# Clustered attention and two expert stages on one core: where the turned sums, the epsilon, the similarity transpose and the first weight conversions are issued

## The chip, the cores and the metric

The kernel runs on one core of one Trainium2 chip. The metric is the device time of one execution in microseconds, taken as the median of several runs. The engines have their usual names here: TensorE (PE, with PEld for its weight loads), VectorE (DVE), ScalarE (ACT), GpSimd (POOL) and SyncE (SP), whose queue issues the DMAs.

## The reference, cut to what matters

```python
B, H, S, D, clusters = 2, 8, 768, 64, 16
q_assign = argmax(einsum('bhsd,hcd->bhsc', q_n, c_n))     # the same for k
mask     = q_assign[..., None] == k_assign[..., None, :]
scores   = where(mask, q @ k.T / sqrt(D), -1e9)
attn     = exp(scores - max(scores))
attn     = attn / (sum(attn) + 1e-9)
x        = (attn @ v) as (1536, 512)
h        = ((x @ w1) * (x @ w2)) @ w3 @ w_out             # first expert stage
out      = (sigmoid(h @ w_gate) * (h @ w_val)) @ w_out2   # second expert stage
```

The weights arrive as 64-bit words and are turned into two-part 32-bit operands on the chip.

## The kernel before

Attention comes first and takes about the first third of the time. Its unit is the head pair: two heads of one batch element, so there are 8 pairs (`pr`, 0 to 7). A pair is cut into 6 blocks (`at`, 0 to 5), each of 256 queries of one head, and a block into two halves of 128 queries. One turn of the loop over `i` issues one block. It is a software pipeline: the turn of block `i` computes the score products of the tiles `2i+3` and `2i+4`, transposes the exponentials of block `i`, and makes the weighted sum of block `i-1`. The pair's twelve row sums come from the exponentials.

All engines run an order written out by hand (`manual_schedule`): each engine and each DMA queue executes what concerns it in the order of the calls in the loop's body, and waits where an operand or a buffer isn't ready. In each half of a block TensorE makes a score product (lines 312 to 315), transposes of exponentials (343) and weighted sums (384, 385). VectorE takes a row maximum (322) and makes the low parts of the transposed exponentials by a subtraction (372). ScalarE computes the exponentials (333), copies the high parts (361, or 358 where GpSimd makes the split, in blocks 1, 2 and 4), and moves a finished weighted sum out (393).

In PSUM there are two score tiles of 1024 columns, of which scores fill 768; three transpose tiles; and one tile for the weighted sum. The similarity product of a coming pair (`prep_sims`, line 242) borrows a score tile, and `rp`, the turned sums of a pair (line 412), a transpose tile.

Between these, the next pair is prepared a step at a time: similarities of queries and keys to the centroids (242), their transpose by VectorE (`prep_sum`, 248), the sum of their halves by GpSimd (`prep_add`, 254), maximum, code (267) and one-hot rows (274, 275), their transpose (279), and in block 3 `prep_mask`: GpSimd turns the key half into 0 or a large negative number (290), and SP moves the rows into QH and KH, the operands of the next pair's first score product, which is issued in the second half of block 4. Then GpSimd adds the head halves of the pair before (432), SP spreads its inverse sums, and GpSimd normalises in block 5. In blocks 3 and 4 the operands of the pair after the next are split (210, 212, 56, 59).

The pair's sums get an epsilon from ScalarE and a reciprocal from VectorE (`invert`, 407, 408, second half of block 4), a transpose by TensorE (`turn_sums`, 413, first half of block 5), and a copy and a store (`store_sums`, 419, 420, end of block 5).

The first four weight matrices (`w_f`, `w_a`, `w`) are converted during attention, each in four steps behind its load: ScalarE 93 and 94 with GpSimd 96; VectorE 102; VectorE 105 with GpSimd 106; ScalarE 108 with GpSimd 111. `CONVERT` says in which pair and block a step is issued, in all cases at the end of the block's second half. They are, as (pair, block): matrix 0 (1,1) (1,3) (1,5) (2,1); matrix 1 (2,3) (3,1) (3,3) (3,5); matrix 2 (4,1) (4,3) (4,5) (5,1); matrix 3 (5,3) (6,1) (6,3) (6,5).

Of the kernel before, what the change touches and what calls it, by code (L numbers as in the profile page):

```python
# [8 lines left out]
F32 = mybir.dt.float32  # L9
F32R = mybir.dt.float32r  # L10
U32 = mybir.dt.uint32
AF = mybir.ActivationFunctionType
# [3 lines left out]
B, H, S, D, C = 2, 8, 768, 64, 16  # L16
NP = H // 2
KT = S // 128
# [9 lines left out]
def tile_cluster_attention__then__moe__then__gated_moe(  # L28
# [15 lines left out]
    nc = tc.nc  # L44
# [4 lines left out]
    NPR = B * NP  # L49
# [69 lines left out]
    ps_t = att.enter_context(tc.tile_pool(name="ps_t", bufs=3, space=PSUM))  # L119
# [125 lines left out]
    def prep_sum(pr):  # L245
        sp = opnd.pop((pr, "sims"))
        sT = core.tile([128, S // 32, 32], F32, tag="raw", name=f"sT{pr}", bufs=3)
        nc.vector.transpose(out=sT.rearrange("p j c -> p (j c)"), in_=sp[:, 0:S])
        opnd[pr, "sT"] = sT
# [44 lines left out]
    def prep_v(pr, e):  # L294
        vx = core.tile([128, KT, 2, D], F32R, tag="vx", name=f"vx{pr}_{e}", bufs=3)
        split(raw[pr, "v"][:, e], vx[:, :, e, :], vx[:, :, 1 - e, :], nc.gpsimd, nc.gpsimd)
        opnd[pr, e, "v"] = vx
# [3 lines left out]
    NB = len(blocks)  # L301
    sps, nms, exps, pts, pcs, phs, avs, acc_x = {}, {}, {}, {}, {}, {}, {}, {}

    def scores(j):

        if not 0 <= j < 2 * NB:
            return
        pr, e, q0 = blocks[j // 2]
        QH, KH, QX, KX = opnd[pr, e]
        q = slice(q0 + 128 * (j % 2), q0 + 128 * (j % 2) + 128)  # L310
        sp = ps_s.tile([128, 1024], F32, tag="s", name=f"s{j}")
        nc.tensor.matmul(sp[:, 0:512], QH[:, q], KH[:, 0:512], start=True, stop=False)
        nc.tensor.matmul(sp[:, 512:S], QH[:, q], KH[:, 512:S], start=True, stop=False)
        nc.tensor.matmul(sp[:, 0:512], QX[:, q], KX[:, 0:512], start=False, stop=True)
        nc.tensor.matmul(sp[:, 512:S], QX[:, q], KX[:, 512:S], start=False, stop=True)  # L315
        sps[j] = sp

    def maxima(j):
        if j not in sps:
            return  # L320
        nms[j] = core.tile([128, 1], F32, tag="nm", name=f"nm{j}", bufs=4)
        nc.vector.tensor_reduce(out=nms[j], in_=sps[j][:, 0:S], axis=AX.X, op=ALU.max, negate=True)  # L322

    def exponentials(j):

        if j not in sps:
            return
        pr, e, q0 = blocks[j // 2]
        at = e * KT + q0 // 128 + j % 2
        if at == 0:  # L330
            acc_x[pr, "sum"] = core.tile([128, 2 * KT], F32, tag="ss", name=f"ss{pr}", bufs=2)
        et = core.tile([128, S], F32, tag="e", name=f"e{j}", bufs=5)
        nc.scalar.activation(et, sps.pop(j)[:, 0:S], AF.Exp, bias=nms.pop(j), accum_out=acc_x[pr, "sum"][:, at : at + 1])  # L333
        exps[j] = et
# [11 lines left out]
    def by_pool(i, k2):  # L346

        return k2 == 0 and i % 6 in (1, 2, 4)
# [15 lines left out]
    def split_lo(i, k2):  # L364
        if (i, k2) not in pts:
            return
        src = pts.pop((i, k2))
        ph, pl = phs[i, k2]
        if by_pool(i, k2):
            split(src, ph, pl, nc.gpsimd, nc.gpsimd)  # L370
        else:
            nc.vector.tensor_tensor(out=pl, in0=src, in1=ph, op=ALU.subtract)  # L372
# [31 lines left out]
    def invert(pr):  # L404

        ss = acc_x[pr, "sum"]
        nc.scalar.activation(ss, ss, AF.Copy, bias=1e-9)
        nc.vector.reciprocal(ss, ss)

    def turn_sums(pr):  # L410

        rp = ps_t.tile([128, 2, 256], F32, tag="t", name=f"rp{pr}")[0 : 2 * KT, 0, 0:128]
        nc.tensor.transpose(rp, acc_x.pop((pr, "sum")), ident)
        acc_x[pr, "rp"] = rp

    def store_sums(pr):
        rp = acc_x.pop((pr, "rp"))
        rt = core.tile([2 * KT, 128], F32, tag="rt", name=f"rt{pr}", bufs=1)
        nc.vector.tensor_copy(rt, rp)
        nc.sync.dma_start(r_dram[pr], rt)  # L420
# [75 lines left out]
    def convert(n):  # L496

        next(steps[n], None)

    CONVERT = {}  # L500
    slots = [(pr, at) for pr in range(1, NPR - 1) for at in ((1, 3, 5), (1, 3, 5), (1, 3))[pr % 3]]
    for n, slot in enumerate(slots[:16]):
        CONVERT[slot] = n // 4
    manual = ExitStack()
    manual.enter_context(tc.manual_schedule(engines={mybir.EngineType.PE, mybir.EngineType.DVE, mybir.EngineType.Activation, mybir.EngineType.Pool, mybir.EngineType.SP}))
    if True:
        for e in range(2):
            prep_v(0, e)
        for i in range(-2, NB + 2):
            pr, at = divmod(i, 6)  # L510
            nxt = pr + 1 if 0 <= i and pr + 1 < NPR else None
            later = nxt + 1 if nxt and nxt + 1 < NPR else None
            late = nxt == 1

            scores(2 * i + 3)
            split_hi(i - 1, 2)
            transposes(i, 0)
            if i == NB - 1:
                turn_sums(pr)
            maxima(2 * i + 3)  # L520
            if i == NB - 1:
                store_sums(pr)
            if nxt and at == 1 + late:
                prep_code(nxt)
            if nxt and at == 1:
                prep_scatter(nxt, 1)
            if later and at == 0:
                load_qk(later)
            if at == 2 and 0 < pr and i < NB:
                join_x(pr - 1)  # L530
            split_lo(i - 1, 2)
            split_hi(i, 0)
            split_lo(i, 0)
            if nxt and at == 3:
                for e in range(2):
                    prep_mask(nxt, e)
            if 0 < pr and i < NB and at == 5:
                norm_x(pr - 1)
                split_x(pr - 1)
            if nxt and at == 2:  # L540
                prep_v(nxt, 0)
            if 0 < pr and i < NB and at == 3:
                add_x(pr - 1)
                spread(pr - 1, "xb", 1)
            exponentials(2 * i + 3)
            if later and at == 3:
                halves = prep_split(later)
                next(halves)
            if later and at == 4:
                for _ in halves:  # L550
                    pass
            weighted_v(i - 1, 0)
            weighted_v(i - 1, 1)
            if 0 <= i < NB - 1 and at == 5:
                turn_sums(pr)
            if i == 0:
                prep_scatter(1, 0)
            if later and at == 5:
                prep_scatter(later, 0)
            if at == 0 and pr < 4:  # L560
                convert(pr)

            scores(2 * i + 4)
            if nxt and at == 0 and not late or i == 1:
                prep_add(nxt)
            if 0 < pr < NPR and at == 0:
                prep_v(pr, 1)
            if nxt and at == 0:
                load_v(nxt)
            transposes(i, 1)  # L570
            split_hi(i, 1)
            weighted_v(i - 1, 2)
            transposes(i, 2)
            take_x(i - 1)
            maxima(2 * i + 4)
            split_lo(i, 1)
            exponentials(2 * i + 4)
            if 0 <= i < NB and at == 4:
                invert(pr)
            if 0 <= i < NB - 1 and at == 5:  # L580
                store_sums(pr)
            if i == -2:
                halves = prep_split(1)
                next(halves)
            if i == -1:
                for _ in halves:
                    pass
            if i == 0:
                prep_sims(1)
                prep_sum(1)  # L590
            if nxt and at == late:
                prep_argmax(nxt)
            if nxt and at == 1 + late:
                prep_onehot(nxt)
            if nxt and at == 2:
                prep_turn(nxt)
            if (pr, at) in CONVERT:
                convert(CONVERT[pr, at])
            if later and at == 5:
                prep_sims(later)  # L600
                prep_sum(later)
            if i == NB - 2:
                end_move(0)
            if i == NB:
                end_move(1, FIRST)
                spread(END, "raw", 3)
                end_add(0)
        end_move(1, LAST)
        end_add(1, FIRST)
        end_norm(FIRST)  # L610
        end_split(FIRST)
        end_add(1, LAST)
        end_norm(LAST)
        end_split(LAST)
# [16 lines left out]
    slots = 0  # L631
# [10 lines left out]
    at = 0.0  # L642
# [118 lines left out]
    late, stage = {}, {}  # L761
# [268 lines left out]
    for M in range(MG // GS):  # L1030
        first = {5 + i: [(M - 1, i)] for i in range(6)} if M else {}
# [113 lines left out]
```

## Time and profile before

| | |
|---|---|
| time, median of 3 runs | 772.67 us (772.16 to 772.98) |
| the profiled execution's own time | 774.57 us |
| its span | 772.8 us |
| TensorE busy | 752.9 us, 97% |
| VectorE busy | 577.3 us, 75% |
| ScalarE busy | 468.9 us, 61% |
| GpSimd busy | 409.8 us, 53% |

The profile is of one execution. The span runs from its first to its last instruction. Busy shares are means over stages of different kinds: attention ends at about 248 us, and only there do VectorE and ScalarE come close to being full. Start times in a row are microseconds from the span's start. Square brackets at the end of a row tell how long the engine sat idle before the instruction and what released it.

### The profile page before, as it was taken

The numbers are of one execution on the slowest core, as the hardware profiler recorded it, in microseconds if no ns is written. First come the engines' busy times: TensorE is split into PE (matmuls) and PEld (weight loads), VectorE is DVE, ScalarE is ACT, GpSimd is POOL, SyncE is SP. The second block draws the span as 40 slices with busy tenths as digits, with TensorE's granted clock in tenths as the row PEclk, the third lists the DMA queues.
The fourth block names the chain that finished last, engine by engine and source line by source line (L and its number), as shares of the span: only waits on it lengthen the run. The fifth ranks groups of instructions, "written<-read, shape, count | busy, mean of one in ns | idle before, by whom it ended". The sixth has DMA issues, their size and how long they took to land.

```text
span 772.8 us, 12258 instructions
## 1 busy us (share of the span) xinstructions
PE 752.9 (97%) x4293; PEld 683.8 (88%) x4293; DVE 577.3 (75%) x895; ACT 468.9 (61%) x980; POOL 409.8 (53%) x418
## 2 busy tenths in 40 slices
PE   8899999999999999999999999899999999999998
PEld 7889888988998888888888999899999999999996
DVE  6799989998987666658663386757577877869674
ACT  2889788889796555455541354676756455564630
POOL 3447777877775355434231137574755647475520
PEclk9999999999999999999999999999999999999999
DMA  8867776756622443333330001130302213031004
GB/s 219 204 169 187 200 191 169 179 157 178 148 73 70 143 147 111 137 136 111 131 141 1 1 1 54 59 107 27 111 27 82 83 55 111 0 113 51 28 1 163
DMA packets 28894, 82.64 MB, mean 107 GB/s; under 512 B 4800, under 2 KB 4960, under 8 KB 28832
## 3 DMA queue, kind: packets, MB, share of 16 engines
q1 hardware_dynamic: 28832, 81.86, 35.6%
q8 instruction: 34, 0.56, 0.3%
q14 instruction: 28, 0.23, 0.1%
HBM read 52.49 MB, written 3.19 MB: 72 GB/s over the span
## 4 chain that ended last, share of the span: by engine, by line
PE 79%; DVE 8%; ACT 6%; issue 3%; POOL 2%; DMA 1%; SPq 0%; ACTq 0%; DVEq 0%; POOLq 0%
PE p L66 12%; PE p L67 12%; PE p L65 12%; PE pt L343 4%; PE p_a L65 4%; PE p_a L66 4%; PE p_a L67 4%; ACT e L333 2%; PE av L385 2%; DVE nm L322 2%; PE av L384 2%; PE p_b L65 2%; PE p_b L66 2%; PE p_b L67 2%; ACT ph L361 2%
## 5 line engine op out<-in xcount | busy, mean ns | idle before, releaser
L333 ACT ACTIVATE e<-s,nm 128x768 f32<-128x768 f32 x96 | 87.9, 916 | 17.3 <-DVE nm L322 15.8
L322 DVE TENSOR_REDUCE nm<-s 128x1 f32<-128x768 f32 x96 | 90.1, 939 | 4.5 <-PE s L315 4.5
L343 PE MATMUL pt<-ident,e 128*128 128x128 f32 x576 | 87.3, 275 | 2.4 <-DVE pl L372 2.4
L372 DVE TENSOR_TENSOR pl<-pt,ph 128x512 fp32r<-128x512 f32 x120 | 80.0, 682 | 10.0 <-ACT ph L361 8.0
L384 PE MATMUL av<-ph,vx 128*128 128x256 f32 x288 | 81.3, 308 | 0.1
L66 PE MATMUL p<-x,w 128*128 128x512 f32 (+1 forms) x208 | 80.0, 385 | 0.0
L65 PE MATMUL p<-x,w 128*128 128x512 f32 (+1 forms) x208 | 80.0, 385 | 0.0
L67 PE MATMUL p<-x,w 128*128 128x512 f32 (+1 forms) x208 | 80.0, 385 | 0.0
L361 ACT CAST ph<-pt 128x512 fp32r<-128x512 f32 x120 | 69.5, 598 | 15.8 <-PE pt L343 15.2
L385 PE MATMUL av<-pl,vx 128*128 128x256 f32 x288 | 74.7, 289 | 4.1 <-DVE pl L372 3.8
L343 PEld LDWEIGHTS pt<-ident,e 128*128 128x128 f32 x576 | 68.3, 142 | 8.4 <-PE s L315 4.2
L106 POOL TENSOR_TENSOR w_a<-w_f 128x512 uint32<-128x512 uint32 x32 | 34.8, 1086 | 62.1 <-DVE w_f L105 26.4
L1024 DVE TENSOR_TENSOR acc<-p,acc 128x512 f32<-128x512 f32 x60 | 41.2, 687 | 29.9 <-PE p L67 29.7
L931 ACT COPY s<-p_a 128x384 f32<-128x384 f32 x72 | 34.4, 480 | 44.2 <-PE p_a L67 43.9
L385 PEld LDWEIGHTS av<-pl,vx 128*128 128x128 f32 x288 | 54.6, 189 | 6.9 <-DVE pl L372 6.3
L855 POOL TENSOR_TENSOR wgv_a<-wgv_f 128x512 uint32<-128x512 uint32 x24 | 25.3, 1055 | 63.4 <-DVE wgv_f L854 43.2
L67 PE MATMUL p<-wo,u 128*128 128x512 f32 x144 | 57.0, 396 | 0.0
L66 PE MATMUL p<-wo,u 128*128 128x512 f32 x144 | 56.7, 394 | 0.0
L65 PE MATMUL p<-wo,u 128*128 128x512 f32 x144 | 56.0, 389 | 0.0
L384 PEld LDWEIGHTS av<-ph,vx 128*128 128x128 f32 x288 | 54.4, 189 | 1.4 <-issue 0.5
L65 PEld LDWEIGHTS p<-x,w 128*128 128x128 f32 x208 | 39.0, 188 | 7.5
L67 PEld LDWEIGHTS p<-x,w 128*128 128x128 f32 x208 | 39.0, 188 | 7.4
(232 smaller groups left out, 2304.3 us busy)
## 6 DMA issues: line engine op xcount, KB each, us to landing
wgv_f<-in_w_gv_dram SPq DMA_DIRECT2D x24, 512.0 KB, 3.2
wo_f<-in_w_out_dram SPq DMA_DIRECT2D x20, 512.0 KB, 3.3
w_f<-in_w_dram SPq DMA_DIRECT2D x16, 512.0 KB, 4.8
w_f<-in_w3T_dram SPq DMA_DIRECT2D x16, 512.0 KB, 3.9
raw<-in_qkT_dram SPq DMA_DIRECT2D x16, 384.0 KB, 3.2
vraw<-in_v_dram SPq DMA_DIRECT2D x8, 384.0 KB
QH<-hi SPq DMA_DIRECT2D x16, 192.0 KB, 4.5
KH<-hi SPq DMA_DIRECT2D x16, 192.0 KB, 3.7
```

The source lines that it names most:

```text
L65: nc.tensor.matmul(ps, whi, xhi, start=start, stop=False, skip_group_check=more)
L66: nc.tensor.matmul(ps, whi, xlo, start=False, stop=False, skip_group_check=more)
L67: nc.tensor.matmul(ps, wlo, xhi, start=False, stop=stop, skip_group_check=more)
L106: nc.gpsimd.tensor_tensor(out=a, in0=high, in1=low, op=ALU.add)
L322: nc.vector.tensor_reduce(out=nms[j], in_=sps[j][:, 0:S], axis=AX.X, op=ALU.max, negate=True)
L333: nc.scalar.activation(et, sps.pop(j)[:, 0:S], AF.Exp, bias=nms.pop(j), accum_out=acc_x[pr, "sum"][:, at : at + 1])
L343: nc.tensor.transpose(pt[:, kk, 128 * t : 128 * t + 128], exps[2 * i + t][:, k0 : k0 + 128], ident)
L361: nc.scalar.copy(ph, pt)
L372: nc.vector.tensor_tensor(out=pl, in0=src, in1=ph, op=ALU.subtract)
L384: nc.tensor.matmul(avs[i], w, ph[:, kk, :], start=kt == 0, stop=False)
L385: nc.tensor.matmul(avs[i], w, pl[:, kk, :], start=False, stop=kt == KT - 1)
L1024: nc.vector.tensor_tensor(out=acc[:, t, :], in0=bk, in1=acc[:, t, :], op=ALU.add)
```

## The change

`invert` is cut in two. The epsilon (`guard_sums`) is issued in the first half of block 4, behind that half's exponential, and the reciprocal stays in the second half. `turn_sums` gets its room from the caller: for all pairs but the last it is columns 768 to 895 of the score tile `2i+4`, and it is issued in the second half of block 5, behind that tile's score product; `store_sums` follows the maximum of that tile. The similarity transpose (`prep_sum`) moves from the end of the block of its product into the first half of the next block, behind the subtraction of the block before and ahead of the maximum. The conversion steps of matrix n are issued at (pair n+2, block 0, second half), (n+2, block 1, second half), (n+2, block 3, first half) and (n+3, block 2, first half). In a first half they stand behind the low part of the block's first transposes and ahead of `prep_mask` and `prep_v`.

```diff
     def invert(pr):
 
         ss = acc_x[pr, "sum"]
+        nc.vector.reciprocal(ss, ss)
+
+    def guard_sums(pr):
+        ss = acc_x[pr, "sum"]
         nc.scalar.activation(ss, ss, AF.Copy, bias=1e-9)
-        nc.vector.reciprocal(ss, ss)
-
-    def turn_sums(pr):
-
-        rp = ps_t.tile([128, 2, 256], F32, tag="t", name=f"rp{pr}")[0 : 2 * KT, 0, 0:128]
+
+    def turn_sums(pr, room):
+
+        rp = room[0 : 2 * KT]
         nc.tensor.transpose(rp, acc_x.pop((pr, "sum")), ident)
         acc_x[pr, "rp"] = rp
...
     CONVERT = {}
-    slots = [(pr, at) for pr in range(1, NPR - 1) for at in ((1, 3, 5), (1, 3, 5), (1, 3))[pr % 3]]
-    for n, slot in enumerate(slots[:16]):
-        CONVERT[slot] = n // 4
+    for n in range(4):
+        for slot in ((n + 2, 0, 1), (n + 2, 1, 1), (n + 2, 3, 0), (n + 3, 2, 0)):
+            CONVERT[slot] = n
...
             transposes(i, 0)
             if i == NB - 1:
-                turn_sums(pr)
+                turn_sums(pr, ps_t.tile([128, 2, 256], F32, tag="t", name=f"rp{pr}")[:, 0, 0:128])
+            first = nxt and at == late
+            if first:
+                split_lo(i - 1, 2)
+                prep_sum(nxt)
             maxima(2 * i + 3)
...
             split_lo(i - 1, 2)
             split_hi(i, 0)
             split_lo(i, 0)
+            if (pr, at, 0) in CONVERT:
+                convert(CONVERT[pr, at, 0])
             if nxt and at == 3:
                 for e in range(2):
                     prep_mask(nxt, e)
...
             exponentials(2 * i + 3)
+            if 0 <= i < NB and at == 4:
+                guard_sums(pr)
...
             weighted_v(i - 1, 1)
-            if 0 <= i < NB - 1 and at == 5:
-                turn_sums(pr)
...
             scores(2 * i + 4)
+            turning = 0 <= i < NB - 1 and at == 5
+            if turning:
+                turn_sums(pr, sps[2 * i + 4][:, S : S + 128])
...
             maxima(2 * i + 4)
+            if turning:
+                store_sums(pr)
             split_lo(i, 1)
             exponentials(2 * i + 4)
             if 0 <= i < NB and at == 4:
                 invert(pr)
-            if 0 <= i < NB - 1 and at == 5:
-                store_sums(pr)
...
                 prep_sims(1)
-                prep_sum(1)
...
-            if (pr, at) in CONVERT:
-                convert(CONVERT[pr, at])
+            if (pr, at, 1) in CONVERT:
+                convert(CONVERT[pr, at, 1])
             if later and at == 5:
                 prep_sims(later)
-                prep_sum(later)
```

## Rows read from the trace of the kernel before

**Rows 1.** The page's first line.
```profile
span 772.8 us, 12258 instructions
```
**Rows 2.** Busy time by pair, 1 to 6; columns: length, engines (x instructions), clock, DMA.
```profile
52.65:80.47 27.82, 27.29 (x204) 25.34 (x202) 26.11 (x38) 24.53 (x54) 19.80 (x19) 1.00 0.75 198
80.47:110.09 29.62, 28.28 (x203) 25.46 (x202) 26.79 (x37) 25.12 (x55) 23.13 (x22) 1.00 0.70 185
110.09:139.15 29.06, 27.39 (x204) 25.31 (x203) 27.20 (x38) 23.60 (x52) 21.24 (x20) 1.00 0.71 189
139.15:168.50 29.35, 27.44 (x204) 25.36 (x202) 27.68 (x38) 25.13 (x55) 22.66 (x21) 1.00 0.66 169
168.50:197.03 28.53, 27.61 (x204) 25.34 (x203) 25.69 (x37) 25.19 (x55) 22.11 (x21) 1.00 0.67 174
197.03:222.37 25.34, 25.30 (x195) 23.83 (x194) 24.11 (x35) 20.81 (x47) 18.51 (x19) 1.00 0.46 118
```
**Rows 3.** TensorE's waits, whole span: us in total, times, longest us.
```profile
PE pt L343 <- DVE pl L372: 2.4, 6, 0.4
```
**Rows 4.** TensorE's timeline, pair 6, blocks 4 and 5: start, length, instruction.
```profile
213.85 0.48 PE L312 MATMUL s<-KH,QH 96*128 96x512 f32 x1
...
216.02 0.40 PE L312 MATMUL s<-KH,QH 96*128 96x512 f32 x1
...
217.99 0.48 PE L312 MATMUL s<-KH,QH 96*128 96x512 f32 x1
```
**Rows 5.** TensorE's timeline, pair 3, from block 4 to the next pair.
```profile
129.09 0.40 PE L312 MATMUL s<-KH,QH 96*128 96x512 f32 x1
...
131.58 0.39 PE L385 MATMUL av<-pl,vx 128*128 128x256 f32 x1 [1.07 <-DVE pl L372]
...
136.38 0.63 PE L343 MATMUL pt<-ident,e 128*128 128x128 f32 x4 [0.43 <-DVE pl L372]
...
137.66 0.70 PE L242 MATMUL sims<-hi,cw 128*128 128x512 f32 x2
...
139.15 0.40 PE L312 MATMUL s<-KH,QH 96*128 96x512 f32 x1
```
**Rows 6.** VectorE's timeline, pair 3, blocks 3 and 4.
```profile
125.84 0.67 DVE L372 TENSOR_TENSOR pl<-pt,ph 128x512 fp32r<-128x512 f32 x1
126.44 0.94 DVE L322 TENSOR_REDUCE nm<-s 128x1 f32<-128x768 f32 x1
...
128.19 1.87 DVE L105 SCALAR_TENSOR_TENSOR w_f<-w_f,w_a 128x512 uint32<-128x512 uint32 x1
...
134.60 0.23 DVE L408 RECIPROCAL ss<-ss 128x12 f32<-128x12 f32 x1 [0.56 <-ACT ss L407]
```
**Rows 7.** VectorE's timeline, pair 5, block 3.
```profile
184.59 0.94 DVE L322 TENSOR_REDUCE nm<-s 128x1 f32<-128x768 f32 x1
```
**Rows 8.** Line 105 in attention: duration ns min/median/max, first and last start us.
```profile
L105 DVE SCALAR_TENSOR_TENSOR w_f<-w_f,w_a x4: 727/1496/2200, 79.9 to 214.8; 128x512 uint32<-128x512 uint32 x4
```
**Rows 9.** GpSimd's timeline, pair 3, blocks 3 and 4.
```profile
124.64 0.83 POOL L290 TENSOR_SCALAR ohT<-ohT 64x768 f32<-64x768 f32 x1 [0.53 <-DVE ohT L279]
127.67 1.84 POOL L432 TENSOR_TENSOR xa<-xa,xb 128x768 f32<-128x768 f32 x1 [2.20 <-DMA xa<-xa]
130.14 1.04 POOL L106 TENSOR_TENSOR w_a<-w_f 128x512 uint32<-128x512 uint32 x1 [0.63 <-DVE w_f L105]
```
**Rows 10.** SP's timeline, pair 3, block 3.
```profile
125.50 0.95 SPq L62 DMA_DIRECT2D KH<-ohT  x1
```
**Rows 11.** That DMA among the issues: size, us from issue to landing.
```profile
KH<-ohT SPq DMA_DIRECT2D x1, 96.0 KB, 2.7
```
**Rows 12.** All moves into KH in attention, mask rows and others.
```profile
DMA to landing us min/median/max: 2.1/2.7/5.2
```
**Rows 13.** Instructions on the turned sums: duration ns min/median/max, first and last start.
```profile
L413 PE MATMUL rp<-ident,ss x8: 269/269/270, 48.7 to 243.6; 128*12 128x128 f32 x8
L419 DVE COPY rt<-rp x8: 268/269/279, 51.8 to 243.9; 12x128 f32<-12x128 f32 x8
```

## The prediction

> **What bounds the kernel now.** The change lies in the attention stage alone, so I read that stage by head pair. In an undisturbed pair TensorE sets the pace: in pair 6 a first half of a block lasts 2.17 us from score product to score product and a second half 1.97 [rows 4], so six blocks want 24.84, and the whole pair takes 25.34 [rows 2]. Pairs 1 to 5 each also hold one similarity product in their last block; it costs 1.49 us, from its first matmul to the next score product [rows 5]. They should therefore take about 26.36, but they take 27.82 to 29.62, and TensorE's busy time falls short of the stretch by 0.5 to 1.9 us [rows 2]. The list of TensorE's waits names VectorE's subtraction (line 372) as the releaser of the weighted sums and, six times, of a transpose [rows 3]. VectorE is busy 25.7 to 27.7 us in those pairs [rows 2]: it has as much work as TensorE, so a stall of VectorE in a block where it is behind appears on TensorE soon after.
>
> Pair 3 shows where. From the second half of its block 4 to the next pair's start TensorE takes 139.15 - 129.09 = 10.06 us. Undisturbed it would be 1.97 + 2.17 + 1.97 + 1.49 = 7.60 [rows 4, 5]. Two waits stand in it: 1.07 us for a subtraction, and 0.43 at the transposes of block 5, which lack a buffer because the turned sums hold one of three [rows 5]. Behind the first stands VectorE: its conversion step at line 105 took 1.87 us, while GpSimd ran line 432 until 127.67 + 1.84 = 129.51 [rows 6, 9]; the same instruction takes between 0.73 and 2.20 [rows 8]. Then the reciprocal waits 0.56 us for the epsilon, which ScalarE issues behind an exponential [rows 6].
>
> **The change part by part.** All times are first of the profiled execution, 774.57 us, of which 772.8 is the span [rows 1] and 1.77 lies around it; it is 1.90 above the median of the runs, 772.67. I take the same difference off both.
>
> *Epsilon one half earlier.* The instruction count stays. VectorE's 0.56 us a pair [rows 6] goes, since the epsilon then stands ahead of a copy, a move and an exponential that the reciprocal used to wait for. What it gives on TensorE is part of the two sums below.
>
> *Sums into the score tile.* The transpose and the copy stay (0.27 each [rows 13]); the transpose buffer stays free, so the wait of up to 0.4 once in six pairs [rows 3] ends. Nothing else waits for the columns: the reciprocal is ready half a block before. The copy now stands ahead of one subtraction, 0.27 on VectorE in block 5, where the similarity product leaves it idle. Its price is zero with that cover and at most 0.27 a pair without it. The store's DMA is issued earlier on SP and nobody waits.
>
> What the rows show is that turn and copy are short; they cannot show two engines on one half of a score tile. The Trainium skill, page "PSUM — Partial Sum Buffer", section "PSUM bank collisions raise a hardware error", asks to guard by bank and quadrant and not by address: columns 768 to 895 lie in the bank of columns 512 to 767, so the maximum would have to wait for the turn, and the exponential for the copy. By that the sum would rise as in the fourth rival; no run here shows it yet.
>
> *Similarity transpose (line 248) one block later.* Before, it blocked VectorE until the similarity product was done, with a subtraction and a maximum behind it. Now the subtraction of block 5 (0.60 from its start to the next instruction's, 125.84 to 126.44 [rows 6]) runs while that product is still going, so VectorE is 0.6 us further on when the next pair begins. The maximum behind it comes 0.6 later; the exponential it feeds has until the second score product after, about 4 us. Zero there.
>
> *First conversions.* Sixteen steps in pairs 1 to 6 become sixteen in pairs 2 to 6. The two VectorE steps now lie in pairs 2 to 5, one set each, in block 1 and in block 3. Line 105 stands in the first half of block 3, before GpSimd's long addition is queued, so it costs 0.73 instead of up to 2.20 [rows 8]. That is the gain. The loss is on GpSimd's queue: line 106, which needs line 105's result, is now **ahead of line 290**, which makes the key half of the next pair's mask. Behind line 290 waits SP's move of that mask into KH, and behind that the first score product of the next pair, in the second half of block 4. Today line 290 starts at 124.64 [rows 9] and the move at 125.50 [rows 10]; it lands 2.7 later [rows 11], at 128.2, 0.9 ahead of the score product at 129.09 [rows 5]. There are only 0.9 us to lose.
>
> The other moved steps issue no DMA. In block 0 ScalarE's two (lines 93, 94) stand ahead of block 1's copies, and GpSimd's line 96 ahead of the code product (line 267) and of the weights that GpSimd splits for block 1; in block 2 ScalarE's line 108 stands ahead of an exponential and GpSimd's line 111 ahead of the split of v, which the next pair needs. They are the same instructions as before, then behind second halves of other blocks. I cost the move at nothing, as ScalarE and GpSimd have idle time (25 and 22 us busy of 29 [rows 2]); without that cover it makes VectorE late, and that is the upper bound of the next paragraph.
>
> New arrival, counted from the pair's start. VectorE reaches the slot of line 105 (the end of the second subtraction of block 3's first half) at 126.44 in pair 3, which starts at 110.09: 16.35 us [rows 2, 6]. In pair 5 it is 184.59 - 168.50 = 16.09 [rows 2, 7]. The moved subtraction takes 0.6 off pair 3's: **15.75**. I bound it by 15.3 (VectorE catching up where it waits for ScalarE) and 16.35 (two conversion steps of ScalarE, now in block 0, give the 0.6 back). Add line 105 with its hand-over, 0.73 + 0.08 = 0.81 [rows 6, 8, 9]; line 106, 1.04 [rows 9]; line 290 up to the move, 0.86 [rows 9, 10]; the landing, between the least of all KH moves and this one, 2.1 to 2.7 [rows 11, 12], taken as 2.4, since these are the smaller of the KH moves. The score product then starts 20.86 us into the pair. Undisturbed it would start at 4 x 4.14 + 2.17 = 18.7 [rows 4]; TensorE stalls for about 2.2 us.
>
> What is late next? During that stall VectorE and ScalarE finish what they owe, and neither the epsilon nor the buffer holds block 5 any more, so the rest is taken at its undisturbed 7.60. A pair then takes 20.86 + 7.60 = 28.46; with the low ends 15.3 + 2.71 + 2.1 + 7.60 = 27.71, with the high ends 29.36. Pairs 2 to 5 took 29.62 + 29.06 + 29.35 + 28.53 = 116.56 [rows 2]; they become 113.84: **-2.7** (-5.7 to +0.9).
>
> Pair 1 has no conversion step left and its mask is not delayed. It took 27.82 against 26.36; I leave 0.6 us for GpSimd's late share of the block-5 weights: 27.0, **-0.8** (-0.4 to -1.4). Pair 0 loses its wait for the transpose buffer: **-0.4** (0 to -0.6). Pair 6 takes 25.34 against 24.84 and keeps one conversion step of three: **-0.2** (0 to -0.5). After attention TensorE has its work queued; nothing is added or taken there.
>
> Sum: -2.7 - 0.8 - 0.4 - 0.2 = **-4.1**: the profiled execution would become 770.5 us, the median 768.6.
>
> **The rivals.**
>
> *First: the mask holds nobody up.* If VectorE reaches line 105 two microseconds earlier, or SP and the DMA are quicker than any move seen, TensorE runs pairs 2 to 5 in about 27.0, as pair 1. That is -8.6 there and -10.0 in all, 762.7. For it speaks only that VectorE gains 0.56 and 0.6 a pair; against it stands that in pair 3 the move would be issued at 110.09 + 15.75 + 2.71 = 128.55 instead of 125.50, 3.0 us later, with 0.9 to lose.
>
> *Second: slower, by a slow mask.* The 2.1 to 2.7 were measured with the move early in block 3. One block later it shares the DMA engines with other moves, and the longest KH move took 5.2 [rows 12]. With that, a pair takes 15.75 + 2.71 + 5.2 + 7.60 = 31.26, the four 125.0, which is +8.5, and +7.1 in all: 779.8. It turns the sign once the landing takes more than 3.4 us, and passes 0.2% at 3.8.
>
> *Third: VectorE still sets block 4 and 5.* If the later line 105 and the subtraction with line 212 leave it 0.8 us behind after each stall, pairs 2 to 5 give back 3.2: -0.9 in all, 771.8.
>
> *Fourth: the score tile is guarded as a whole.* Maximum after turn and exponential after copy: 0.27 + 0.27 [rows 13] in each of seven pairs, 3.8 us if nothing covers it: -0.3, 772.4. Cover is there: the exponential stands behind two ScalarE instructions that wait for TensorE's transposes, so I give it little.
>
> **How the numbers follow.** Forecast 0.62, first rival 0.12, second 0.09, third 0.11, fourth 0.06. Predicted is the forecast's 768.6. With every term at its low end it gives -5.7 - 1.4 - 0.6 - 0.5 = -8.2, with every term at its high end +0.9 - 0.4 = +0.5: 764.5 to 773.2. That takes in the third and fourth rival and leaves out the first two, 0.21 between them, so it is the range. A measurement of this kernel can tell about 0.2%, 1.55 us, from no change. Faster by more, under 771.1: nearly all of the forecast and the first rival, and a little of the third, 0.72. Within: the rest of these and the fourth, 0.17. Slower: the second and the tail of the third, 0.11.
>
> **What would show it.** In the new trace, GpSimd's line 290 of pairs 2 to 5 should start behind line 106, some 3 us later in the pair; TensorE should show a wait of about 2 us at the score product of block 4's second half, released by a DMA, four times. Line 105 should take 0.73. The reciprocal's wait of 0.56 and the 0.4 at the transposes should be gone, and pair 1 should take about 27.0. The prediction is wrong if that score product starts on time, if a landing takes over 3.4 us, or if block 5 still runs much above its undisturbed 2.17 + 1.97 + 1.49 = 5.63.

## The result: slower, and where the time is in the profile after

The changed kernel takes 778.68 us in the median (777.07 to 782.06) against 773.25 us (772.16 to 775.73) of the kernel before on the same chip: ratio 1.0070, interval 1.0054 to 1.0085. The forecast was 768.6, with 773.2 as the upper end, and 0.11 for slower. The sign was wrong. The profiled execution of the changed kernel took 782.06 us, 3.4 above its median; its span is 780.0 against 772.8 [rows 1]. It is the slowest of the six runs and the one with the lowest mean granted clock, 0.987 (the fastest, 777.07, had 0.996), so the trace may show more of the clock's cost than the median holds.

The page's first line, and busy time by pair, 1 to 6, in the changed kernel (columns as in [rows 2]):

```profile
span 780.0 us, 12244 instructions
```

```profile
52.41:79.36 26.95, 26.95 (x204) 25.21 (x202) 25.40 (x36) 23.24 (x52) 17.91 (x17) 1.00 0.73 195
79.36:110.82 31.46, 28.84 (x203) 26.93 (x202) 27.01 (x38) 24.99 (x54) 24.23 (x22) 0.95 0.70 184
110.82:140.48 29.66, 27.15 (x203) 25.29 (x202) 27.02 (x38) 25.00 (x55) 22.24 (x21) 1.00 0.71 183
140.48:171.91 31.43, 28.76 (x203) 26.81 (x202) 27.00 (x38) 25.35 (x55) 24.10 (x22) 0.95 0.64 160
171.91:203.39 31.48, 28.55 (x203) 26.59 (x202) 27.02 (x38) 25.18 (x55) 23.19 (x21) 0.95 0.63 158
203.39:229.42 26.03, 25.19 (x195) 23.91 (x194) 23.62 (x34) 21.17 (x48) 16.92 (x17) 1.00 0.45 115
```

Pairs 2 to 5 take 124.03 instead of 116.56 [rows 2], +7.5; pair 1 takes 0.9 less, pair 6 0.7 more, and pair 7 starts 7.05 later than before. So the whole difference of the spans, 7.2, is made in attention, nearly all of it in the four pairs in which a line 105 stands ahead of the mask. VectorE's busy time in the four is 108.1, against 107.4 before. What is new in the clock column is the 0.95 in three of the four.

TensorE's waits, whole span (us in total, times, longest):

```profile
PE s L312 <- DMA KH<-ohT: 5.4, 3, 2.4
PE s L312 <- ACT hi L56: 2.6, 1, 2.6
...
PE av L385 <- DVE pl L372: 2.2, 6, 0.9
PE s L312 <- ACT ss L411: 2.2, 1, 2.2
```

The waits for a transpose buffer [rows 3] are gone. In their place the score product (line 312) waits for the mask's move into KH, in pairs 2, 4 and, 0.84 us, 6. Pairs 3 and 5 have the same wait under a ScalarE name. The score product can't need line 56, for in pair 4 that line (161.99 to 162.82, below) ends after the score product began at 162.54; and line 411 is the epsilon, which no score product reads. Pair 4, from block 3 to the next pair: GpSimd, VectorE, SP, ScalarE, then TensorE.

```profile
153.41 1.28 POOL L111 TENSOR_TENSOR w<-w_a,w 128x512 fp32r<-128x512 f32 x1
...
158.13 1.04 POOL L106 TENSOR_TENSOR w_a<-w_f 128x512 uint32<-128x512 uint32 x1 [1.85 <-DVE w_f L105]
159.26 0.83 POOL L290 TENSOR_SCALAR ohT<-ohT 64x768 f32<-64x768 f32 x1
```

```profile
157.37 0.67 DVE L105 SCALAR_TENSOR_TENSOR w_f<-w_f,w_a 128x512 uint32<-128x512 uint32 x1
```

```profile
160.12 0.54 SPq L62 DMA_DIRECT2D KH<-ohT  x1
```

```profile
161.99 0.83 ACT L56 CAST hi<-raw 128x768 fp32r<-128x768 f32 x1
```

```profile
162.54 0.47 PE L312 MATMUL s<-KH,QH 96*128 96x512 f32 x1 [2.35 <-DMA KH<-ohT]
...
165.91 0.76 PE L312 MATMUL s<-KH,QH 96*128 96x512 f32 x1
...
168.37 0.40 PE L312 MATMUL s<-KH,QH 96*128 96x512 f32 x1
...
171.91 0.40 PE L312 MATMUL s<-KH,QH 96*128 96x512 f32 x1
```

GpSimd sat idle for 1.85 us, up to 158.13, with line 290's operands ready (VectorE's line 279, which makes them, ended at 155.41), because line 106 is ahead of it and waits for line 105. The move is issued at 160.12 and TensorE starts at 162.54, 2.42 later. What then follows is a second loss: the half behind the wait takes 165.91 - 162.54 = 3.37 instead of 1.97 [rows 4]. The granted clock in that half, in pairs 2 to 5 (columns as in the table by pair):

```profile
101.40:105.20 3.80, 3.72 (x17) 3.56 (x18) 2.21 (x4) 1.57 (x4) 3.72 (x3) 0.55 0.77 209
132.70:134.80 2.10, 2.08 (x17) 2.00 (x17) 1.41 (x3) 1.05 (x3) 2.02 (x2) 1.00 0.59 176
162.50:166.00 3.50, 3.46 (x17) 3.34 (x17) 2.04 (x4) 1.46 (x4) 3.42 (x3) 0.59 0.73 205
194.20:197.70 3.50, 3.46 (x17) 3.30 (x17) 1.30 (x3) 0.81 (x3) 3.42 (x3) 0.57 0.83 218
```

After its wait TensorE ran three of these halves mostly at 1.2 GHz (0.55 to 0.59 granted), and one, in pair 3, at 2.4. Before the change the clock is 1.00 in each of pairs 1 to 6 [rows 2]. Set against the prediction, counted from each pair's start:

| | line 105 | move issued | score product | from there to the next pair |
|---|---|---|---|---|
| predicted | 15.75 | 18.46 | 20.86 | 7.60 |
| pair 2 | 17.12 | 19.86 | 22.12 | 9.34 |
| pair 3 | 16.88 | 19.62 | 21.90 | 7.76 |
| pair 4 | 16.89 | 19.64 | 22.06 | 9.37 |
| pair 5 | 16.88 | 19.62 | 22.33 | 9.15 |

The four pairs came out 124.03 - 113.84 = 10.2 above the forecast: 5.0 because the score product starts later (4.8 of it is line 105's slot), and 5.2 in the rest of the pair (4.6 of it in the half behind the wait).

### The profile page after: what moved, and what is told of

Same layout as the page of the kernel before. It is cut to its first block, busy times and chain, and to the rows that moved or that the text cites. A ratio compares the mean times of both kernels' runs of the same rounds, so it can differ in the third digit from the quotient of the medians.

```text
span 780.0 us, 12244 instructions
## 1 busy us (share of the span) xinstructions
PE 755.8 (97%) x4293; PEld 688.9 (88%) x4293; DVE 575.9 (74%) x895; ACT 468.6 (60%) x980; POOL 409.9 (53%) x418
## 4 chain that ended last, share of the span: by engine, by line
PE 77%; DVE 7%; ACT 5%; issue 4%; POOL 4%; DMA 2%; SPq 0%; POOLq 0%; ACTq 0%; DVEq 0%
PE p L66 12%; PE p L67 12%; PE p L65 12%; PE p_a L66 4%; PE p_a L65 4%; PE p_a L67 4%; PE pt L343 4%; PE p_b L65 2%; PE p_b L66 2%; PE p_b L67 2%; ACT e L333 2%; PE av L385 2%; PE av L384 2%; PE w34p L66 2%; PE w34p L67 2%
## 5 line engine op out<-in xcount | busy, mean ns | idle before, releaser
L343 PE MATMUL pt<-ident,e 128*128 128x128 f32 x576 | 89.1, 279 | 0.0
L343 PEld LDWEIGHTS pt<-ident,e 128*128 128x128 f32 x576 | 70.7, 145 | 4.4
L312 PE MATMUL s<-KH,QH 96*128 96x512 f32 x96 | 43.8, 456 | 12.3 <-DMA KH<-ohT 5.4
L66 PEld LDWEIGHTS p<-x,w 128*128 128x128 f32 x208 | 39.0, 188 | 7.5
```

Source lines behind the costliest of these rows:

```text
L66: nc.tensor.matmul(ps, whi, xlo, start=False, stop=False, skip_group_check=more)
L343: nc.tensor.transpose(pt[:, kk, 128 * t : 128 * t + 128], exps[2 * i + t][:, k0 : k0 + 128], ident)
```

## The experiments

The theory after the comparison (Q): the loss is the mask's place in GpSimd's queue, and the clock that falls behind the wait. Each expectation names its rival. Edits are against the changed kernel unless another is named, and ratios are to the kernel before on the same chip.

### The mask ahead of the conversion step

```diff
-            if (pr, at, 0) in CONVERT:
-                convert(CONVERT[pr, at, 0])
             if nxt and at == 3:
                 for e in range(2):
                     prep_mask(nxt, e)
+            if (pr, at, 0) in CONVERT:
+                convert(CONVERT[pr, at, 0])
```

> Theory Q (the mask's place in GpSimd's queue): the changed kernel loses its time where line 106 stands ahead of the mask step (line 290), 10.0 us at the score product of block 4's second half in pairs 2 to 5, and 4.6 us in the half after it, where TensorE runs at the lower clock in three of the four pairs. Here the conversion call of a first half stands behind the mask instead of ahead of it; nothing else moves. Q expects the mask to be about 1 us late in pairs 3 to 6 (line 111 is still ahead of it, as in pair 6 of the changed kernel, 1.0 us) and in time in pair 2, no half at the lower clock, and the kernel at 767 to 772 us. Rival V (VectorE is behind in blocks 3 to 5 and the mask only shows it): TensorE then waits for VectorE's subtraction in block 4 instead, and the kernel stays above 775.

Measured: 769.18 us against 774.17, ratio 0.9942 (0.9922 to 0.9962). Its pair 3: busy time, GpSimd, SP, TensorE.

```profile
107.58:135.68 28.10, 27.43 (x202) 25.41 (x201) 26.34 (x38) 24.96 (x55) 23.08 (x22) 1.00 0.76 196
```

```profile
123.72 0.84 POOL L290 TENSOR_SCALAR ohT<-ohT 64x768 f32<-64x768 f32 x1
125.53 1.04 POOL L106 TENSOR_TENSOR w_a<-w_f 128x512 uint32<-128x512 uint32 x1 [0.98 <-DMA xa<-xa]
```

```profile
124.58 0.55 SPq L62 DMA_DIRECT2D KH<-ohT  x1
```

```profile
127.36 0.46 PE L312 MATMUL s<-KH,QH 96*128 96x512 f32 x1
```

The score product follows 2.78 us behind the move and waits no more, also in pairs 3 and 5, where the wait had a ScalarE name; the clock is 1.00. Pairs 2 to 5 take 28.10 to 28.16. So moving two lines further down is worth 1.3% (1.0070 to 0.9942), and turns the sign. Q holds; a remaining wait of the mask showed in pair 6 alone (0.4 us), less than I had expected.

### The new slots alone, and the three other edits alone

Slots alone is the kernel before with the new CONVERT; the other three alone is the changed kernel with the old one:

```diff
-    for n in range(4):
-        for slot in ((n + 2, 0, 1), (n + 2, 1, 1), (n + 2, 3, 0), (n + 3, 2, 0)):
-            CONVERT[slot] = n
+    slots = [(pr, at) for pr in range(1, NPR - 1) for at in ((1, 3, 5), (1, 3, 5), (1, 3))[pr % 3]]
+    for n, slot in enumerate(slots[:16]):
+        CONVERT[(*slot, 1)] = n // 4
```

> The kernel before with the new conversion slots alone. If the parts add up it is slower than before by what the whole change costs plus what the other three parts give, about 5.4 + 5.6 = 11 us: 782 to 786. The rival that the late mask hides VectorE's waits in blocks 4 and 5 (the three parts then have nothing left to give) expects 778 to 780, as the whole change.

> The changed kernel with the conversion steps at their old slots: epsilon, turned sums and similarity transpose alone. Q expects block 5 of pairs 0 to 5 to run as in the changed kernel (5.7 us instead of 6.7), the mask in time, and 766 to 770 us. The rival that the moved similarity transpose costs what the other two give expects 772 to 774.

Slots alone: 778.46 us against 774.17, ratio 1.0068 (1.0045 to 1.0091), as slow as the whole change: the rival's figure, so the parts don't add. Its score products in pair 3, from the waiting one on:

```profile
133.94 0.74 PE L312 MATMUL s<-KH,QH 96*128 96x512 f32 x1 [2.21 <-ACT e L333]
...
137.56 0.48 PE L312 MATMUL s<-KH,QH 96*128 96x512 f32 x1
...
139.76 0.48 PE L312 MATMUL s<-KH,QH 96*128 96x512 f32 x1
...
143.29 0.40 PE L312 MATMUL s<-KH,QH 96*128 96x512 f32 x1
```

Behind the wait and the slow half (3.62) block 5 takes 2.20 + 3.53 = 5.73, though the epsilon, the turned sums and the transpose are where they were before. The stall itself clears what the three edits were to clear, so in pairs 2 to 5 they have almost nothing left to give: 123.69 us here, 124.03 with all four parts.

The three others alone: 773.11 us, ratio 0.9996 (0.9978 to 1.0015), no change; I had expected 766 to 770. Pairs 1 to 5 take 143.54 together, 0.8 less than before [rows 2], and pair 6 0.75 more, 26.09. With the old slots VectorE is late elsewhere, in the second half of block 4 (2.60 to 2.83) and in the first of the next pair's block 0 (2.61 or 2.62 in three pairs).

### The slots with the mask first, without the other three

> The kernel before with the new conversion slots and the mask ahead of the step: the first experiment without epsilon, turned sums and similarity transpose. If these three parts carry the gain of the first experiment (block 5 in 6.3 instead of 6.8 us, six times, and the reciprocal's wait), this one is 3 to 4 us slower than it: 772 to 773.5. The rival that the slots alone carry the gain, because line 105 no longer waits for GpSimd, expects 768.5 to 770.5.

The edit is the first experiment's, on the kernel with the slots alone. Measured: 771.27 us against 774.43, ratio 0.9959 (0.9943 to 0.9975), between the two expectations. So most of the gain of 0.58% is the slots', and the three edits add about 0.17%, though the intervals overlap. Pair 3:

```profile
109.43:137.86 28.43, 27.59 (x204) 25.36 (x202) 26.35 (x38) 25.09 (x55) 22.74 (x22) 1.00 0.74 195
```

That is 0.33 longer than with the three edits. The second half of block 5 is 4.13 to 4.16 here, as before, and 3.65 with them. Since it stays at 3.65 with the transpose at its old place (below), that half microsecond is the sums' and the epsilon's.

### Keeping TensorE busy through the wait

```diff
-    def scores(j):
+    def scores(j, idle=0):
...
+        for _ in range(idle):
+            nc.tensor.transpose(sp[:, S : S + 128], ident, ident)
...
-            scores(2 * i + 4)
+            scores(2 * i + 4, 20 if at == 4 and 2 <= pr <= 5 else 0)
```

Twenty useless transposes into unused columns stand ahead of the score product that waits; the mask is as late as in the changed kernel.

> The changed kernel plus 20 transposes of the identity into the unused columns of the score tile, ahead of the score product that waits for the mask, in pairs 2 to 5: some 2.2 us of useless work for TensorE in a stall of 2.2 to 2.6. Theory C (the half behind the stall takes 3.4 to 3.6 us instead of 2.0 because TensorE is granted the lower clock after its stall) expects the granted clock at 1.0 there, that half at 2.0 to 2.1, and 773.5 to 775.5 us. The rival that this half is long because buffers or VectorE's results are late expects no change or a loss, 778 to 780.

Measured: 775.25 us against 774.17, ratio 1.0009 (0.9994 to 1.0025), where the changed kernel has 1.0070: added work makes it faster, into the range that theory C expected. Pair 4, the transposes (line 313 here), the score product (314), and the window behind:

```profile
159.14 2.37 PE L313 MATMUL s<-ident 128*128 128x128 f32 x20
161.39 0.47 PE L314 MATMUL s<-KH,QH 96*128 96x512 f32 x1
```

```profile
162.00:166.00 4.00, 4.00 (x33) 3.83 (x33) 3.36 (x6) 3.20 (x7) 3.49 (x3) 1.00 0.75 202
```

The half behind now takes 2.03 to 2.08 in all four pairs, at a granted clock of 1.00. The slow halves are the clock's, and the clock fell because TensorE stood still. Of the 1.28% that the mask's place costs (1.0070 against 0.9942) they are 0.61, a little under half; in the traces pairs 2 to 5 take 124.03 us, 119.38 with the transposes and 112.52 with the mask first.

### The early steps of the conversion, in the changed kernel and with the mask first

```diff
-        for slot in ((n + 2, 0, 1), (n + 2, 1, 1), (n + 2, 3, 0), (n + 3, 2, 0)):
+        for slot in ((n + 2, 0, -1), (n + 2, 1, 1), (n + 2, 3, 0), (n + 3, 2, 0)):
...
             split_hi(i - 1, 2)
+            if (pr, at, -1) in CONVERT:
+                convert(CONVERT[pr, at, -1])
             transposes(i, 0)
```

> The first experiment (mask ahead of the conversion step) with the first conversion step (lines 93, 94, 96) issued at the start of block 0, behind the copy of the block before, where ScalarE sits idle for 1.1 us, instead of at the end of block 0. Theory S (what is left over 4.14 us a block in blocks 1 and 2 of pairs 2 to 5, 0.4 and 0.55 us, comes from this step, which stands ahead of the copies and, on GpSimd, of the code product) expects these halves at 1.97 to 2.1 and 765 to 767.5 us. The rival that VectorE's own work is the bound in these blocks (moved transpose, maximum and code steps) expects no change against the first experiment, 768.5 to 770.

> The changed kernel (mask still behind line 106) with one edit: ScalarE's lines 93 and 94 and GpSimd's 96 stand at the start of block 0 instead of its end. It asks how much of the late arrival at line 105 (16.88 us into the pair, the prediction had 15.75) comes from these steps. Theory Q, the place of the mask is what costs and step 1 is a small part: with step 1 early and the mask first the slot was 16.64, so here the score product of block 4's second half starts 0.2 to 0.5 us earlier in each of four pairs, while TensorE itself arrives 0.5 earlier, so its wait stays at 2.2 to 2.7 us and the granted clock still falls behind it: 776.5 to 778. Rival, step 1 is what made the slot late beyond the prediction's bound: slot at 16.1 or less, waits under 1.8 us and the clock stays up: 770 to 773.

With the mask first: 767.87 us against 774.43, ratio 0.9915 (0.9895 to 0.9934); pairs 2 to 5 take 27.61 to 27.67 instead of 28.10 to 28.16, since the second halves of blocks 1 and 2 fall from 2.41 and 2.53 to 2.15 and 2.30. Theory S had expected 1.97 to 2.1 in both, so this step is only a part of it. The 0.3 that is left in block 2 shows in pairs 2 to 5 alone, which have line 102 just ahead of it; pairs 1 and 6 take 1.98 and 1.97 there. No run moves line 102. With the mask still late: 780.33 us against 773.99, ratio 1.0077 (1.0061 to 1.0094), no better than the changed kernel. Line 105 comes 0.45 to 0.47 earlier in the four pairs (16.41 there instead of 16.89 in pair 4), the score product likewise, and it waits as long as before. Pair 4, and the clock behind its wait:

```profile
163.15 0.47 PE L312 MATMUL s<-KH,QH 96*128 96x512 f32 x1 [2.39 <-DMA KH<-ohT]
...
166.30 0.77 PE L312 MATMUL s<-KH,QH 96*128 96x512 f32 x1
...
168.97 0.40 PE L312 MATMUL s<-KH,QH 96*128 96x512 f32 x1
```

```profile
163.15:166.30 3.15, 3.15 (x16) 3.06 (x17) 1.88 (x4) 1.31 (x4) 3.07 (x3) 0.63 0.72 205
```

I had expected 776.5 to 778. The place of the wait moved as expected, but what came earlier was lost behind it: here all four pairs lost clock, and the slow stretch reached into block 5, whose first half took 2.26 to 2.96.

### The similarity transpose at its old place

Here `prep_sum` goes back behind `prep_sims`, once with the mask first and once with the mask first and the early step:

```diff
-            first = nxt and at == late
-            if first:
-                split_lo(i - 1, 2)
-                prep_sum(nxt)
...
                 prep_sims(1)
+                prep_sum(1)
...
                 prep_sims(later)
+                prep_sum(later)
```

> The first experiment with the similarity transpose back at its old place. The prediction gave the move 0.6 us a pair, six pairs, so 3.6 us slower by it: 772 to 773. The theory that VectorE idles as long at the new place, since the subtraction ahead of it waits 0.94 us for ScalarE's copy, expects no difference: 768.5 to 770.

> Mask first and step 1 early, and in addition the similarity transpose (line 248) back at its old place. The prediction priced the move of that transpose at a gain of 0.6 us a pair. Theory T, the move costs 0.2 a pair: with it block 1's second half takes 2.15 us, and it should be 1.98 without it in pairs 1 to 6, so pairs 2 to 5 take 27.4 instead of 27.64 and the median comes out 0.8 to 1.2 us below that of the kernel with the transpose moved, near 767. Rival, the prediction: without the move the maximum and the subtraction behind the transpose are late, +0.6 in five pairs, near 771.

With the mask first: 769.06 us against 774.43, ratio 0.9929 (0.9908 to 0.9951), the same as with the transpose moved. With the early step too: 765.74 us against 773.99, ratio **0.9898** (0.9882 to 0.9914), the best version of all; its interval overlaps that of the early step alone (0.9915), so the price of the move is read from the pairs. Pairs 1 and 3 of the best one:

```profile
51.71:78.48 26.77, 26.75 (x204) 25.14 (x202) 25.41 (x36) 23.38 (x52) 18.60 (x18) 1.00 0.79 206
...
105.89:133.32 27.43, 27.18 (x203) 25.33 (x202) 26.31 (x38) 25.05 (x55) 23.30 (x22) 1.00 0.77 201
```

Pair 3 is 0.18 shorter than with the transpose moved (27.61), in the other couple 0.22 (27.88 and 28.10), and pair 1 is 0.18 to 0.2 shorter. With the mask first, the move costs 0.2 us a pair. The start of pair 4 shows how, in the kernel before and in the changed kernel:

```profile
139.35 0.98 DVE L248 STREAM_TRANSPOSE sT<-sims 128x768 f32<-128x768 f32 x1 [0.75 <-PE sims L242]
```

```profile
140.71 0.69 DVE L372 TENSOR_TENSOR pl<-pt,ph 128x512 fp32r<-128x512 f32 x1 [0.94 <-ACT ph L361]
141.31 0.97 DVE L248 STREAM_TRANSPOSE sT<-sims 128x768 f32<-128x768 f32 x1
```

Before, the transpose itself waited 0.75 us for the similarity product. Now the subtraction that was to fill this gap waits 0.94 us for its operand from ScalarE. VectorE idles at least as long as it did, and transposes 0.63 later in the pair (0.83 behind its start instead of 0.20).

### The last step at the end of block 3

> Mask first and step 1 early, and in addition the last conversion step (ScalarE line 108, GpSimd line 111) at the end of block 3 instead of the first half of block 2, so that 1.25 us of GpSimd's work leaves the queue ahead of the mask (line 290). Theory Q, any GpSimd work ahead of the mask delays it: the first half of block 4 in pair 6, 2.50 us, and in pair 5, 2.36, come back to 2.17, and block 2's second half, 2.30, to about 2.0: 1 to 2 us less, 766 to 767. Rival, the step only moves its cost: line 111 then delays the split of block 4's weights and the weighted sum there waits: 768 to 770.

> All of it together: mask first, step 1 early, last step at the end of block 3, similarity transpose at its old place. If the parts add: 0.8 to 1.2 us below the kernel with the step late alone, 765 to 766.5. If they share the same slack: no better than the better one of the two, 766 to 767.

The slot `(n + 3, 2, 0)` becomes `(n + 3, 3, 1)`; the second kernel has the transpose back as well. Measured: 770.84 us, ratio 0.9957 (0.9942 to 0.9972), and 769.63 us, 0.9946 (0.9928 to 0.9965). Both are worse than without this edit, so Q's expectation failed. In the first, pair 2, which has no last step, stays at 27.62, and pairs 3 to 5 take 28.50 to 28.75. GpSimd and TensorE in pair 3, block 4:

```profile
126.97 1.29 POOL L111 TENSOR_TENSOR w<-w_a,w 128x512 fp32r<-128x512 f32 x1
128.22 1.34 POOL L54 TENSOR_SCALAR ph<-pc 128x512 fp32r<-128x512 f32 x1
129.64 1.26 POOL L59 TENSOR_TENSOR pl<-pc,ph 128x512 fp32r<-128x512 f32 x1
```

```profile
130.96 0.38 PE L385 MATMUL av<-pl,vx 128*128 128x256 f32 x1 [0.44 <-POOL pl L59]
```

Line 111 now delays GpSimd's split of block 4's weights, and the weighted sum waits for it: the rival's reason. GpSimd's queue is tight behind the mask as well as ahead of it. Pair 6 of the first shows something else: line 111 is out of the mask's way there too and the move is issued at 207.75, 15.29 into the pair, a microsecond earlier than in the changed kernel (16.27); yet the score product waits, 4.65 us behind the move:

```profile
212.40 0.47 PE L312 MATMUL s<-KH,QH 96*128 96x512 f32 x1 [1.05 <-DMA KH<-ohT]
```

## Why the prediction was wrong, point by point

**The mechanism was right.** Line 106 ahead of line 290, GpSimd waiting for line 105, the move 3 us later in the pair, TensorE waiting about 2 us for a DMA in four pairs: all of it is in the trace. Line 106, line 290 and the move together took 2.74 from line 105's start, predicted 2.71; from the move to the score product it was 2.26 to 2.71, predicted 2.1 to 2.7. Line 105 took 0.67, predicted 0.73. The reciprocal no longer waits [rows 6], the transposes neither [rows 3].

**The first failed step is the slot of line 105**, 15.75 with an upper end of 16.35. It was 16.88 to 17.12, beyond that end; against 15.75 that is 4.8 us in the four pairs. I had taken 0.6 off pair 3's 16.35 for the moved similarity transpose, and it gained nothing: with the transpose at its old place (the slots alone) line 105 comes at 16.83 to 16.85, so moving the transpose costs 0.04 in pairs 3 to 5 of the changed kernel and 0.28 in pair 2. I had costed step 1 in block 0 at nothing because ScalarE was busy 25 of 29 us; issued earlier in the block, it gives 0.46 back. 16.35 + 0.04 + 0.46 = 16.85. The cover was a mean over the pair, while ScalarE's copies of block 1 are wanted at once: in pair 4 VectorE's subtractions wait 0.16 + 0.30 = 0.46 us for the copies that stand behind lines 93 and 94.

```profile
147.43 0.69 DVE L372 TENSOR_TENSOR pl<-pt,ph 128x512 fp32r<-128x512 f32 x1 [0.16 <-ACT ph L361]
...
149.29 0.69 DVE L372 TENSOR_TENSOR pl<-pt,ph 128x512 fp32r<-128x512 f32 x1 [0.30 <-ACT ph L361]
```

The upper end was wrong in its logic: it let the steps cancel the gain, but not add to a loss.

**The second failed step is "the rest is taken at its undisturbed 7.60".** It was 7.76 where the clock stayed up, and 9.15 to 9.37 where it fell. VectorE and ScalarE did catch up during the wait, as I wrote; block 5 took 5.71 to 6.00 against 5.63. But I asked only what is late after a wait, and not what TensorE itself does after one. The rows that I read had no TensorE wait of two microseconds in attention, so nothing bounded this term; I should have left it open upwards. The measured slot alone takes my sum from -4.1 to +0.7, and the measured rest adds 5.2.

**The smaller terms.** Pair 1 was predicted 27.0 and took 26.95. Pair 0 took 30.54, 0.2 more instead of 0.4 less; in the thirteen traces it took 29.36 to 31.66, so this says little. Pair 6 took 26.03, 0.7 more instead of 0.2 less. There is no line 105 in it, but line 111 stands in block 2 ahead of the mask, and the move is issued 16.27 into the pair instead of 15.39. I had named line 111's place ahead of the split of v and not asked what that does to the mask behind both. Still, that delay isn't the whole reason why the score product waits:

```profile
219.66 0.54 SPq L62 DMA_DIRECT2D KH<-ohT  x1
```

```profile
223.13 0.47 PE L312 MATMUL s<-KH,QH 96*128 96x512 f32 x1 [0.84 <-DMA KH<-ohT]
```

The product starts 3.47 behind the move. In the run with the useless transposes the move is issued as late (16.28), and the product follows 2.47 behind it without a wait; with line 111 out of the way (above) it comes 4.65 behind. So in pair 6 the landing itself is slow in some of the traces, and why stays open.

**The rivals.** The second, a slow landing, gave 779.8, near the measured 778.68, but for another reason: in its four pairs no score product came over 2.71 behind the move. Only in pair 6 did it come later, 3.47. The first, that the mask holds nobody up, is what the kernel becomes when the mask goes first; its 27.0 a pair was 28.1, and 27.4 in the best version. The third did not show: TensorE's waits for the subtraction fell from 3.8 us in all to 2.2. The fourth shows, but small. ScalarE's exponential in block 5 waits for the copy of the turned sums, in the changed kernel in pair 1 alone, with the mask first in pairs 1 to 5; there, in pair 3:

```profile
134.64 0.91 ACT L333 ACTIVATE e<-s,nm 128x768 f32<-128x768 f32 x1 [0.24 <-DVE rt L422]
```

The two touch other columns of one tile, and still the one waits for the other; the price is 0.24 on ScalarE where block 5 isn't already late. The Trainium skill, page "PSUM — Partial Sum Buffer", section "PSUM bank collisions raise a hardware error", asks to guard by bank and not by address; the trace agrees, though no run here tells a guard by bank from one by tile. No wait of the maximum for the turn shows.

**Open:** beside pair 6, why the clock stayed up after two of the twelve waits of 2.2 to 2.6 us (pair 3 of the changed kernel and pair 4 with the slots alone). No run here tells.

## What to carry to other kernels

A step that only fills idle time must not stand ahead of a step with a due time on an in-order queue: find the last consumer that waits on that queue, count its slack in microseconds (here 0.9), and put the filler behind it. Price a wait on TensorE with the slower stretch that follows it, and price a moved step by the block in which it now stands, not by the engine's idle share over a pair. When a prediction's bound is a gain given back, ask whether the same step can cost more than that.

## What the runs showed of the hardware

- After waits of 2.2 to 2.6 us TensorE's granted clock was 0.53 to 0.70 over the next half block in 10 of 12 cases (three kernels), mostly the 1.2 GHz level, and the half took 2.84 to 3.64 instead of 1.97. After the wait of 0.84 in pair 6 the half took 2.04. Twenty useless transposes (2.37 us) in place of the wait kept it at 2.4 (1.00 granted) in all four pairs. The Trainium skill, page "TensorE: Matmul & The Clock Gate", section "What's actually happening", says that the default is throttled and activity releases it; the run with the transposes agrees.
- Line 105 on VectorE took 0.67 with GpSimd idle (157.37, above) and 1.87 while GpSimd was in line 432 until 129.51 [rows 6, 9]. The Trainium skill, page "SBUF — State Buffer", section "Who interferes with whom", says that a VectorE instruction with two SBUF inputs contends with GpSimd's reads; the trace agrees.
- A wait that the trace puts down to a ScalarE instruction was the mask's DMA: with the mask moved and ScalarE's order the same, it was gone.
